# K of two batches mixed by 64x64 blocks in four array tiles, with a new order of work

## The chip, the cores and the metric

The kernel runs on one core of one Trainium2 chip. The metric is the device time of one execution in microseconds (us).

## What is computed

Inputs are q, k, v (4 batches, 8 heads, 768 rows, 64 columns), a sort network (4, 8, 8, 8) and the weights of a gated layer. The reference, cut to what matters:

```python
P = sort_net                                   # (4, 8, 8, 8)
for _ in range(5):
    P = exp(P - max(P)); P = P / (sum over j); P = P / (sum over i)
k_sorted = einsum('bhij,bhjcd->bhicd', P, k in 8 blocks of 96 rows)   # v_sorted likewise
attn = softmax(q_block @ k_sorted_block.T / 8)                        # 8 blocks of 96x96 per head
x = (attn @ v_sorted_block), heads side by side                       # (4, 768, 512)
h = maximum(x @ w_in, 0);  u, v = halves of h                         # 512 columns each
v_s = w_spatial @ layernorm(v) + b_spatial                            # (768 x 768) @ (768 x 512)
out = (u * v_s) @ w_out                                               # (4, 768, 512)
```

## The kernel before

All of the program is one list, `ORDER`, of small units. A unit is a name and its arguments; what it issues goes to the engines' queues in the order of the list, and each engine takes its own queue in order. Nothing is moved by a scheduler. `ps` arguments name the place in PSUM (0 to 3: two banks, 10 to 17: one bank), `A`, `D` and `P` an engine (ScalarE or ACT, VectorE or DVE, GpSimd or POOL). The units that matter here:

- `L` loads a tensor through POOL's DMA queue (`L:wu` and `L:wv` the input weights, L185 and L182, `L:wsa`, `L:wsb` the spatial weights, `L:wo` the output weights).
- `KT` (line 395 in `mixed`) mixes and turns K of one pair of heads: `pd`, a 128x128 matrix per head made on POOL (`PD`, line 293) from the normalised P and a mask, is multiplied with K as it lies in SBUF. Twelve matmuls of 128 columns, 64 array columns each; a copy by ACT or DVE puts the result into `kt_all`. `VM` (line 422) mixes V, `VC` copies it by eight DMAs on SyncE (SP) into `vb`.
- `QP` and `QX` turn q of batches 2 and 3 by a DMA transpose on SP (line 382); batches 0 and 1 are turned on TensorE (PE).
- `SC` (line 454) makes scores on PE (64 array rows) and their exponent on ACT; `AT` (line 500) multiplies with mixed V on PE, and DVE divides (a reciprocal, line 507, and a multiply, line 508). `XD` turns the result by a DMA transpose on SP (line 518), `XT` on PE.
- `VP` and `VH` (line 567) make the v half of the input product and its relu, `VP` in matmuls of 512 columns, `VH` in two of 256. `ST` (lines 587, 588), `LN` and `LA` (line 599) normalise it on DVE. `UP` (line 613) makes the u half.
- `WT`, `WW` turn the spatial weights on PE. `SP` (line 625) and, for batch 3, `SH` (line 681) are the spatial products, whose sum `z` DVE makes; all six normalised tiles of a batch feed each of them. `GT` and `GH` multiply with u on DVE or POOL; `OP` and `OH` (lines 651, 701) are the output products, `OE`, `OI` their copies, `OS`, `OJ` the stores.
- `CK` (lines 731 to 734) tests the sums of the softmax against a range with eleven small DVE operations, `CF` adds up the test on PE, `LF` loads the flag into every engine. `IF` is a branch on it: the rest of the list, or a general path that does not run for these inputs.

The list interleaves the batches: while batch b is in its gated layer, batch b+1 is in its attention.

Of the kernel before, what the change touches and what calls it, by code (L numbers as in the profile page):

```python
# [22 lines left out]
SC:0:0:0:0 L:v:1:0:8 PD:1:0:4 VB:15:D:0:3 SC:3:0:1:0 AT:1:0:2:0 SC:0:0:2:1 AT:2:0:3:0 SC:3:0:0:1 PD:1:4:8 AT:1:0:0:0  # L23
KT:0:A:1:0 XT:14:D:0:0:2 AT:3:0:0:1 SC:1:0:3:1 KT:0:A:1:3 AT:2:0:2:1 VM:1:A:1:0 AT:3:0:3:1 VM:0:A:1:1 VM:2:D:1:3
L:q:1:0:8 VM:1:A:1:2 XT:16:A:0:1:2 L:wv AT:0:0:1:0 XT:17:A:0:1:0 KT:2:D:1:1 KT:1:A:1:2 QT:16:D:1:1 QT:10:D:1:3
QT:11:A:1:2 QT:17:D:1:0 XT:14:D:0:0:0 SC:1:1:1:0 L:wsa SC:0:1:2:1 SC:3:1:2:0 VP:15:D:0:4 ST:0:4 VP:14:D:0:3 L:wu
SC:1:1:0:0 SC:0:1:1:1 VP:15:D:0:1 L:wsb ST:0:3 WT:16:A:1 WT:17:D:0 VP:14:A:0:0 ST:0:1 VH:15:A:0:2 ST:0:0 WT:16:A:2
VC:1:0:4 L:q:2:0:8 VH:17:A:0:5 VC:1:4:8 PD:2:0:4 ST:0:2 ST:0:5 AT:1:1:0:0 LN:0:0:6 AT:0:1:1:0 UP:2:A:0:0:0
UP:3:A:0:1:0 BI LA:0:3 LA:0:4 AT:1:1:2:0 SC:2:1:0:1 UP:0:A:0:1:1 LA:0:1 AT:3:1:2:1 L:v:2:0:8 WT:14:A:3 L:k:2:0:8
LA:0:5 LA:0:2 WW:1:D:4 LA:0:0 SC:0:1:3:1 SC:3:1:3:0 UP:2:A:0:0:1 PD:2:4:8 AT:0:1:3:1 QP:A:2:0 SP:1:0:3 QP:A:2:3  # L30
AT:3:1:3:0 QP:A:2:2 AT:2:1:0:1 QP:A:2:1 SP:0:0:0 AT:1:1:1:1 SP:3:0:2 VM:2:A:2:2 XD:1:0 VM:0:A:2:1 GT:D:0:0 SP:1:0:1
VM:3:D:2:0 GT:P:0:1 VM:2:A:2:3 VH:10:A:1:0 ST:1:0 KT:1:A:2:0 KT:2:D:2:1 KT:3:A:2:3 QX:2:0:4 KT:0:D:2:2 XD:1:1
UP:1:A:1:1:0 VH:16:D:1:1 SC:2:2:2:0 SC:0:2:0:0 VC:2:0:4:0:4 ST:1:1 GT:P:0:2 SC:1:2:3:0 VH:17:D:1:3 L:wo UP:2:A:1:1:1
AT:0:2:2:0 VH:16:A:1:4 AT:1:2:0:0 GT:P:0:3 VH:17:D:1:5 SC:2:2:1:0 L:q:3:0:8 SC:0:2:0:1 SC:1:2:1:1 VH:16:A:1:2 ST:1:3
UP:2:A:1:0:0 ST:1:5 AT:0:2:3:0 ST:1:4 ST:1:2 UP:1:A:1:0:1 LN:1:0:6 OP:3:0:2:2 LA:1:5 LA:1:1 SC:2:2:3:1 L:v:3:0:8
SC:0:2:2:1 PD:3:4:8 LA:1:0 OP:1:0:4:2 PD:3:0:4 LA:1:3 LA:1:2 OE:A:0:2 LA:1:4 L:k:3:0:8 QP:D:3:0 VC:2:4:8:0:4 OE:A:0:4
AT:2:2:3:1 SP:0:1:3 QP:A:3:3 AT:3:2:1:0 AT:1:2:2:1 QP:A:3:1 SP:2:1:1 AT:0:2:1:1 QP:A:3:2 VM:3:A:3:1 OP:1:0:0:2
OE:D:0:0 OS:0:0:0:1:A OS:0:0:1:2:A VM:2:A:3:3 AT:3:2:0:1 SP:0:1:2 VM:1:A:3:0 GT:P:1:1 XD:2:0 VM:3:D:3:2 SP:2:1:0
VH:16:D:2:2 QX:3:0:4 KT:0:A:3:0 KT:1:D:3:2 KT:2:D:3:3 KT:3:A:3:1 XD:2:1 VH:10:D:2:0 SC:1:3:0:1 ST:2:2 SC:3:3:0:0
SC:2:3:3:1 VC:3:4:8:0:4 OS:0:4:0:1 OS:0:4:1:2 VH:11:D:2:4 VH:10:A:2:5 AT:1:3:0:1 GT:P:1:3 VH:16:D:2:3 ST:2:3 ST:2:5  # L40
GT:P:1:2 SC:2:3:1:1 SC:0:3:2:1 SC:1:3:1:0 VH:17:A:2:1 GT:D:1:0 UP:2:A:2:1:0 AT:0:3:2:1 UP:1:A:2:1:1 ST:2:1 AT:3:3:1:1
ST:2:4 AT:2:3:3:1 UP:0:A:2:0:1 ST:2:0 UP:1:A:2:0:0 VC:3:0:4:0:4 AT:3:3:0:0 LN:2:0:6 LA:2:2 OP:0:1:0:2 OE:A:1:0 LA:2:4
AT:2:3:1:0 OP:1:1:4:2 LA:2:5 SC:3:3:2:0 LA:2:0 LA:2:3 LA:2:1 SC:0:3:3:0 OP:2:1:2:2 AT:3:3:3:0 SP:0:2:1 GT:D:2:1
OE:A:1:4 XD:3:1 AT:1:3:2:0 SP:3:2:0 SP:0:2:2 CK XD:3:0 GT:P:2:0 OE:A:1:2 SP:2:2:3 VH:1:D:3:5:3 GT:D:2:3 VH:10:D:3:4
UP:3:A:3:1:1 CF:11 VH:12:A:3:2 VH:13:A:3:1 OS:1:2:0:1 OS:1:2:1:2 LF VH:16:A:3:0 GT:D:2:2 OS:1:0:0:1:A OS:1:0:1:2:A
UP:2:A:3:1:0 ST:3:1 ST:3:3 UP:0:A:3:0:0 ST:3:4 ST:3:5 OP:1:2:0:2 ST:3:2 ST:3:0 OP:3:2:4:2 LN:3:0:6 LA:3:3 OE:D:2:0
LA:3:4 OP:2:2:2:2 LA:3:0 LA:3:1 OE:A:2:2 LA:3:5 UP:0:A:3:0:1 OE:A:2:4 LA:3:2 OS:0:2:0:1 OS:0:2:1:2 SH:12:3:2:0
SH:13:3:3:0 GH:P:3:3:0 SH:16:3:0:0 GH:D:3:2:0 SH:17:3:1:0 GH:P:3:0:0 SH:16:3:1:1 SH:12:3:2:1 OS:2:4 GH:P:3:1:0
SH:13:3:3:1 OS:2:0 GH:D:3:1:1 SH:17:3:0:1 OS:1:4 GH:D:3:3:1 OS:2:2 GH:P:3:0:1 GH:P:3:2:1 IF OH:16:3:2:0:512:0:4
# [19 lines left out]
def kernel(  # L69
# [18 lines left out]
    TB = 128 // NB  # L88
    BH = B * H
# [63 lines left out]
    prep_sb = const.tile([128, NB, BH], BF16, name="prep_sb")  # L153
    vm = const.tile([128, G, H, VW], BF16, name="vm")
# [16 lines left out]
    def u_L(what, *a):  # L171
        if what in ("q", "k", "v"):
# [113 lines left out]

    def u_PC(eng):
        copy(eng, prep_sb, st["pr"])
# [34 lines left out]
    def q_turned(t, b, hp):  # L323
        for g in range(G):
            for hh in range(2):
                nc.tensor.transpose(  # L326
                    t[hh * 64:hh * 64 + 64, g * 128:(g + 1) * 128],
                    st["q", b][:, 2 * hp + hh, g * D:(g + 1) * D], ident)
# [40 lines left out]
    def u_QP(eng, b, hp):  # L369

        b, hp = int(b), int(hp)
        if ("qp", b) not in st:
            st["qp", b] = ld_tile("qp").rearrange("p h c -> p (h c)").rearrange(
                "p (k g h d) -> p k g h d", k=HP, g=G, h=2)
        copy(
            eng, st["qp", b][:, hp].rearrange("p g h d -> p h g d"),
            st["q", b][:, 2 * hp:2 * hp + 2].rearrange("p h (g d) -> p h g d", g=G),
        )
# [23 lines left out]
    def u_KT(ps, eng, b, hp):  # L402
        mixed("k", "kT", ps, eng, int(b), int(hp))

# [41 lines left out]
    def u_SC(ps, b, hp, ih):  # L446
# [3 lines left out]
        for ii in range(NI):  # L450
            i = ih * NI + ii
            for hh in range(2):
                rows = slice(hh * 64, hh * 64 + 64)
# [9 lines left out]
    def u_SM(b, hp, ih):  # L463
# [5 lines left out]
        for ii in range(NI):  # L469
            i = ih * NI + ii  # L470
            for hh in range(2):
                rows = slice(hh * 64, hh * 64 + 64)
# [203 lines left out]
    def u_SH(ps, b, mc, c):  # L676
        b, mc, c = int(b), int(mc), int(c)
        t, x = ps_tile(ps)[:, 0], tokens(c)
        w = x.stop - x.start
        for n in range(G):  # L680
            nc.tensor.matmul(  # L681
                t[:, 0:w], lhsT=st["v_sb", b, n][:, mc * 128:(mc + 1) * 128],
                rhs=wspT[:, x.start // 128:x.stop // 128, n, :],
                start=(n == 0), stop=(n == G - 1),
            )
# [74 lines left out]
    def general_path():  # L760
# [9 lines left out]
        u_PC("A")  # L770
        for b in range(B):
            if b > 0:
                u_PD(b, 0, 8)
            for x in ("q", "k", "v"):
                u_L(x, b, 0, H)
# [3 lines left out]
            for hp in range(HP):  # L779
                u_QN(2, "A", b, hp)  # L780
                u_KT(3, "D", b, hp)
# [67 lines left out]
```

## Time and profile before

| | us |
|---|---|
| runs | 149.42, 150.09, 150.87 |
| median | 150.09 |
| span of the profiled execution, first to last instruction | 147.7 |
| PE busy | 141.4 |
| DVE busy | 115.1 |
| ACT busy | 85.2 |
| POOL busy | 39.1 |

The execution that was profiled has no time of its own listed beside its span; the runs' median is 2.4 us above that span, for what lies around the first and the last instruction. Of a page's lines: PE is TensorE's matmuls, PEld its weight loads, L625 a line of the kernel; a group's row gives its shapes, its count, busy time and mean duration in ns, then the engine's idle time ahead of it and what ended it.

### The profile page before, as it was taken

To read this page: it belongs to the slowest core of one execution; us is meant where nothing else is said; L and a number is where in the kernel's file an instruction comes from. 1 tells how busy PE (TensorE), PEld (TensorE's weight loads), DVE (VectorE), ACT (ScalarE), POOL (GpSimd) and SP (SyncE) were. 2 spreads that over 40 slices of the span, in tenths; PEclk is the share of its full clock that TensorE was granted. 3 is DMA by queue.
4 is the path that set the end of the run, shared out by engine and by line. 5 is a ranking of instruction groups with operands and counts; after the bars stand their busy time and mean duration, and the time that the engine had idled before them with its cause. 6 is when DMAs were issued, how large, how long until landed. Compare 5 with 4: busy or idle time off the path is not lost.

```text
span 147.7 us, 4114 instructions
## 1 busy us (share of the span) xinstructions
PE 141.4 (96%) x1691; PEld 101.0 (68%) x1691; DVE 115.1 (78%) x263; ACT 85.2 (58%) x125; POOL 39.1 (26%) x44
## 2 busy tenths in 40 slices
PE   6997999999999999999999999999999999999991
PEld 2466777857776667776877678768866876854760
DVE  3878899979987978867869879899558989846741
ACT  5357998988789447658793328756640046160040
POOL 6701994410000006991002640000002100004630
PEclk9999999999999999999999999999999999999999
DMA  2999999999999999899999999503602507007856
GB/s 60 278 204 205 204 207 201 208 225 243 227 233 231 204 200 269 131 177 211 206 202 175 213 239 278 132 0 83 28 0 60 190 2 284 0 2 266 307 210 228
DMA packets 37013, 25.93 MB, mean 176 GB/s; under 512 B 16704, under 2 KB 34112, under 8 KB 36992
## 3 DMA queue, kind: packets, MB, share of 16 engines
q0 software_dynamic: 14432, 12.19, 51.9%
q1 hardware_dynamic: 21552, 11.88, 33.8%
q10 hardware_dynamic: 1008, 1.57, 2.8%
q8 instruction: 14, 0.23, 0.6%
q14 instruction: 7, 0.06, 0.1%
HBM read 24.78 MB, written 6.29 MB: 210 GB/s over the span
## 4 chain that ended last, share of the span: by engine, by line
PE 82%; DMA 8%; DVE 5%; POOL 2%; issue 1%; ACT 1%; POOLq 0%; DVEq 0%
PE ps L625 16%; PE ps L567 15%; PE ps L613 14%; PE ps L651 11%; DMA k_in<-in_k_dram 8%; PE ps L681 5%; PE ps L500 4%; PE ps L395 4%; PE ps L701 4%; PE ps L454 4%; PE ps L422 3%; DVE x_sb L508 2%; PE ps L326 1%; PE ps L536 1%; PE ps L530 1%; DVE vb L124 1%
## 5 line engine op out<-in xcount | busy, mean ns | idle before, releaser
L642 POOL TENSOR_TENSOR gt<-z,u_sb 128x768 bf16<-128x768 f32 x7 | 11.4, 1642 | 68.0 <-DVE z L631 54.7
L459 ACT ACTIVATE ex_all<-ps 96x768 bf16<-96x768 f32 x32 | 23.7, 805 | 5.0 <-PE ps L454 4.1
L625 PE MATMUL ps<-wspT,v_sb 128*128 128x384 bf16 x144 | 25.0, 326 | 0.0
L567 PE MATMUL ps<-w_in_sb,xT 128*128 128x256 bf16 (+1 forms) x176 | 23.8, 283 | 0.0
L613 PE MATMUL ps<-xT,w_in_sb 128*128 128x384 bf16 x128 | 23.0, 326 | 0.0
L128 ACT ACTIVATE u_sb<-ps 128x768 bf16<-128x768 f32 x16 | 13.0, 811 | 17.3 <-PE ps L613 17.2
L508 DVE TENSOR_TENSOR x_sb<-ps,rec_all 96x512 bf16<-96x512 f32 x32 | 22.0, 687 | 1.1
L625 PEld LDWEIGHTS <-v_sb 128*128 128x128 bf16 x144 | 13.5, 98 | 8.4
L567 PEld LDWEIGHTS <-xT 128*128 128x128 bf16 x176 | 16.2, 98 | 4.0
L651 PE MATMUL ps<-w_out_sb,gt 128*128 128x256 bf16 x144 | 16.9, 273 | 0.0
L613 PEld LDWEIGHTS <-w_in_sb 128*128 128x128 bf16 x128 | 12.0, 98 | 7.0
L587 DVE BATCH_NORM_STATS2 stats<-v_sb 128x6 f32<-128x512 bf16 x24 | 16.2, 675 | 0.6 <-ACT v_sb L128 0.5
L122 ACT COPY o_sb<-ps 128x1024 f32<-128x1024 f32 (+2 forms) x11 | 8.9, 830 | 12.6 <-PE ps L701 9.3
L631 DVE TENSOR_TENSOR z<-ps,b_bc 128x768 f32<-128x768 f32 x12 | 11.5, 954 | 5.9 <-PE ps L625 5.1
L651 PEld LDWEIGHTS <-gt 128*128 128x128 bf16 x144 | 13.8, 98 | 2.0
L500 PEld LDWEIGHTS <-ex_all 96*128 96x128 bf16 x256 | 11.1, 97 | 2.6
L500 PE MATMUL ps<-vb,ex_all 96*128 96x65 bf16 x256 | 12.4, 193 | 0.1
L122 ACT CAST vm<-ps 128x768 bf16<-128x768 f32 x9 | 6.8, 807 | 9.7 <-PE ps L422 6.6
L694 POOL TENSOR_TENSOR gt<-z,u_sb 128x512 bf16<-128x512 f32 (+1 forms) x5 | 5.2, 1046 | 21.5 <-DVE z L687 21.5
L507 DVE RECIPROCAL rec_all<-ps 96x8 f32<-96x8 f32 x32 | 6.3, 196 | 5.5 <-PE ps L500 5.3
L130 DVE TENSOR_SCALAR v_sb<-ps 128x512 bf16<-128x512 f32 (+1 forms) x12 | 8.7, 727 | 1.7 <-PE ps L567 1.5
L236 PE MATMUL ps<-warm 128*128 128x512 bf16 (+3 forms) x38 | 8.5, 386 | 1.3 <-DVE warm L210 1.3
(100 smaller groups left out, 199.9 us busy)
## 6 DMA issues: line engine op xcount, KB each, us to landing
v_in<-in_v_dram POOLq DMA_DIRECT2D x4, 768.0 KB, 16.0
k_in<-in_k_dram POOLq DMA_DIRECT2D x4, 768.0 KB, 14.9
vb<-vm SPq DMA_DIRECT2D x24, 99.0 KB, 4.8
q_in<-in_q_dram POOLq DMA_DIRECT2D x3, 768.0 KB, 11.6
out_dram<-o_sb SPq DMA_DIRECT2D x9, 256.0 KB, 2.3
out_dram<-o_sb SPq DMA_DIRECT2D x4, 512.0 KB, 5.9
out_dram<-o_sb ACTq DMA_DIRECT2D x5, 256.0 KB, 2.3
ws_in<-in_moe_w_spatial_dram POOLq DMA_DIRECT2D x2, 576.0 KB, 18.9
```

What stands on the lines that cost most here:

```text
L122: nc.scalar.copy(out=out, in_=in_)
L128: nc.scalar.activation(out=out, in_=in_, func=AF.Relu)
L459: nc.scalar.activation(out=e_tile(b, hp, ih).rearrange("p h (x g) -> p h x g", g=G), in_=t[0:BLK, :, 0:HW].rearrange("p h (g x) -> p h x g ...
L500: nc.tensor.matmul(t[:, hh, ii * VW:ii * VW + D + 1], lhsT=e[:, c:c + 128], rhs=vb[b % 2][:, ih * NI + ii, 2 * hp + hh, 0:D + 1], start=Tr ...
L508: nc.vector.tensor_mul(out=x_sb[:, hp].rearrange("p i (h d) -> p h i d", h=2), in0=tv[:, :, :, 0:D], in1=_raw_ap(rec, 0, [rec.ap[0], [NI, ...
L567: nc.tensor.matmul(t[:, x, c:c + DH // parts], lhsT=st["xT", b][:, n // 3, kc, (n % 3) * 128:(n % 3 + 1) * 128], rhs=w_in_sb[:, kc, DH + c ...
L587: nc.vector.bn_stats(out=stats, in_=st["v_sb", b, n])
L613: nc.tensor.matmul(t[:, x, 0:HW], lhsT=w_in_sb[:, kc, mc * 128:(mc + 1) * 128], rhs=st["xT", b][:, ih, kc, :], start=(kc == 0), stop=(kc = ...
L625: nc.tensor.matmul(t[:, x, 0:HW], lhsT=st["v_sb", b, n][:, mc * 128:(mc + 1) * 128], rhs=wspT[:, 3 * x:3 * x + 3, n, :], start=(n == 0), s ...
L631: nc.vector.tensor_add(out=z.rearrange("p (x c) -> p x c", x=2), in0=t[:, :, 0:HW], in1=b_bc.rearrange("p (x c) -> p x c", x=2),)
L642: eng.tensor_mul(out=gt, in0=st["z", b, mc], in1=u)
L651: nc.tensor.matmul(t[:, x, c:c + w], lhsT=st["gt", b, mc][:, (n0 + x) * 128:(n0 + x + 1) * 128], rhs=w_out_sb[:, mc, c:c + w], start=(mc = ...
```

## The change

K of batches 2 and 3 is loaded in another layout: each partition holds 12 rows of one head, the 64 lower partitions an even head, the 64 upper ones an odd head, in 3 KB pieces in place of 1.5 KB. Eight blocks and 8 rows of each are mixed by a 64x64 matrix per head, `pn`, which two new POOL products (`PN`) make. For it stand new units: `M8` (two small POOL operations: a mask and a spread of 8 in place of 16), `PS` (eight matmuls that spread P for the last two batches) and `PY` (their copy by ACT). `KP` takes the place of `KT` there: for two pairs of heads 48 matmuls of 64 rows, 64 array columns and 64 columns each, turn by turn in four 64x64 tiles of the array, and two copies. In these batches odd pairs of heads have their two heads swapped in the partitions (`half`), so that `QP` copies an odd pair in two pieces.

The core of the diff:

```diff
+        if what == "k" and int(a[0]) >= KB:
...
+            nc.gpsimd.dma_start(
+                out=st["k", b][:, lo:hi],
+                in_=_raw_ap(k, (b * H + 2 * lo) * S * D, [[GR * D, 128], [2 * S * D, hi - lo], [1, GR * D]]),
+            )
...
+    def u_M8():
+        nc.gpsimd.tensor_add(out=mask8, in0=m32[:, 0:TR], in1=m32[:, TR:TB])
+        nc.gpsimd.tensor_copy(out=spread8, in_=spread[:, :, 0:TR])
+
+    def u_PS(ps):
...
+        for i in range(NI):
+            for hh in range(2):
+                nc.tensor.matmul(
+                    parts[hh * 64:hh * 64 + 64, i], lhsT=spread8[:, i * NB:(i + 1) * NB].rearrange("p j t -> p (j t)"),
+                    rhs=turned_p[:, hh, :, KB * HP:], start=True, stop=True,
+                )
...
+    def u_PN(b, lo, hi):
...
+        nc.gpsimd.tensor_mul(
+            out=pn(b)[:, lo:hi].rearrange("p h (i t) -> p h i t", t=TR),
+            in0=_raw_ap(mask8, 0, [mask8.ap[0], [0, n], [0, NB], [1, TR]]),
+            in1=_raw_ap(prep8, (b - KB) * HP + lo, [prep8.ap[0], [1, n], [(B - KB) * HP, NB], [0, TR]]),
+        )
+
+    def half(b, hp, hh):
+        lo = 64 * (hh ^ (hp & 1) if b >= KB else hh)
+        return slice(lo, lo + 64)
...
+    def u_KP(ps0, ps1, eng, b, m):
+        b, m = int(b), int(m)
+        ts = [ps_tile(ps0), ps_tile(ps1)]
+        for n in range(GR):
+            for row in range(2):
+                g = (n + G * row) % GR
+                for o in range(2):
+                    rows = slice(64 * row, 64 * row + 64)
+                    nc.tensor.matmul(
+                        ts[o][half(b, o, row), g // G, (g % G) * 64:(g % G) * 64 + 64],
+                        lhsT=st["k", b][rows, 2 * m + o, g * D:(g + 1) * D], rhs=pn(b)[rows, 2 * m + o, :],
+                        start=True, stop=True,
+                    )
+        for o in range(2):
+            to = turned("kT", b, 2 * m + o)[:, 0:S].rearrange("p (x b g) -> p b x g", b=2, g=G)
+            copy(eng[o], to, ts[o][:, :, 0:HW].rearrange("p b (g x) -> p b x g", g=G))
```

(GR = 12, G = 6, KB = 2.) The list `ORDER` is another one from the middle of batch 1's attention on: nearly every unit behind it has another place or another engine. Two of its lines, before and after:

```diff
-VH:16:D:2:2 QX:3:0:4 KT:0:A:3:0 KT:1:D:3:2 KT:2:D:3:3 KT:3:A:3:1 XD:2:1 VH:10:D:2:0 SC:1:3:0:1 ST:2:2 SC:3:3:0:0
+QP:D:3:2 QX:3:0:4 SP:3:1:2 SP:0:1:1 KP:2:3:DA:3:0 GT:P:1:1 VH:12:D:2:0 VH:10:A:2:1 VH:15:A:2:4 VH:14:A:2:2 GT:D:1:2
```

Among the units that change places: the first `UP` of batch 0 stands ahead of its two neighbouring attention products instead of behind them; `XD:2:1`, the second half of batch 2, ahead of `QX:3` instead of behind it; `CK` behind the first V product of batch 3 instead of ahead of it; `L:wo` behind three `GT` on POOL instead of two; DVE has five `UP` copies (none before) and three `GT` in place of five.

On SyncE's queue, before, from batch 2's copies of mixed V on (`vb` is the mixed V, `qT` and `xT` the turned q and attention result):

```order
L435 DMA vb_97<-vm 96x1x528 x8
L518 DMA_TRANSPOSE xT<-x_sb 128x16x96
L382 DMA_TRANSPOSE qT<-qp 128x24x128
L518 DMA_TRANSPOSE xT<-x_sb 128x16x96
L435 DMA vb_98<-vm 96x1x528 x4
L666 DMA out_dram<-o_sb 128x512 x2
L435 DMA vb_98<-vm 96x1x528 x4
```

The same place now:

```order
L505 DMA vb_100<-vm 96x1x528 x8
L588 DMA_TRANSPOSE xT<-x_sb 128x16x96 x2
L435 DMA_TRANSPOSE qT<-qp 128x24x128
L505 DMA vb_101<-vm 96x1x528 x8
L736 DMA out_dram<-o_sb 128x512 x2
```

The turned q of batch 3 went behind the second `xT` of batch 2, and the copies of V are no longer parted by stores.

On DVE, before, from batch 2's last spatial sum (`z`) on, right behind the eleven operations of `CK` (`v_sb` a relu copy of V, `gt` a product with u, the two `ends` and `flag` rows the end of the range check):

```order
L631 TENSOR_TENSOR z<-ps,b_bc 128x768
L130 TENSOR_SCALAR v_sb<-ps 128x1024
L642 TENSOR_TENSOR gt<-z,u_sb 128x768
L130 TENSOR_SCALAR v_sb<-ps 128x512
L748 TENSOR_REDUCE ends<-ps 1x1
L749 CAST flag<-ends 1x1
L752 TENSOR_LOAD flag
L642 TENSOR_TENSOR gt<-z,u_sb 128x768
L587 BN_STATS stats<-v_sb 128x6
L588 BN_AGGR mv<-stats 128x2
```

The same place now, from the V copy of two tiles on, as far as the first operations of `CK`:

```order
L133 TENSOR_SCALAR v_sb<-ps 128x1024
L133 TENSOR_SCALAR u_sb<-ps 128x2x384
L657 BN_STATS stats<-v_sb 128x6
L658 BN_AGGR mv<-stats 128x2
L803 MEMSET bad 128x5
L805 TENSOR_REDUCE ends<-rec_all 96x1
L806 TENSOR_SCALAR bad<-ends 96x1
```

And what stands behind `CK`:

```order
L133 TENSOR_SCALAR v_sb<-ps 128x512
L657 BN_STATS stats<-v_sb 128x6
L658 BN_AGGR mv<-stats 128x2
L133 TENSOR_SCALAR u_sb<-ps 128x2x384
L712 TENSOR_TENSOR gt<-z,u_sb 128x768
```

`CK` and two U copies came in between batch 3's V copies and statistics; one `gt` and the load of the flag went out of this place.

130 lines of the change are left out of this document (81 added, 49 removed).

## The prediction

> **What bounds the kernel now.** I read the page first: its span, its busy times and the shares of its chain.
>
> ```profile
> span 147.7 us, 4114 instructions
> PE 141.4 (96%) x1691; PEld 101.0 (68%) x1691; DVE 115.1 (78%) x263; ACT 85.2 (58%) x125; POOL 39.1 (26%) x44
> PE 82%; DMA 8%; DVE 5%; POOL 2%; issue 1%; ACT 1%; POOLq 0%; DVEq 0%
> ```
>
> TensorE holds 82% of the chain that ended last, but a busy PE need not be a PE at its pace. So I looked in the view of waits for everything PE itself waited for, and then at busy time by stretches (their columns: length, then busy time and count of PE, PEld, DVE, ACT, POOL, then the granted clock, DMA share and GB/s).
>
> ```profile
> PE ps L236 <- DVE warm L210: 1.3, 1, 1.3
> PE ps L413 <- ACT vt_all L122: 0.6, 1, 0.6
> PE ps L267 <- DVE mask L224: 0.5, 1, 0.5
> 90.00:105.00 15.00, 15.00 (x194) 11.61 (x188) 14.00 (x34) 10.14 (x15) 0.00 (x0) 1.00 0.52 99
> 115.00:125.00 10.00, 10.00 (x80) 7.50 (x78) 8.76 (x23) 3.51 (x6) 0.01 (x1) 1.00 0.44 163
> ```
>
> These three are all of PE's own waits, and they belong to the start: warm-up, the mixing weights, the first turn of V. In the stretches shown, as in all between 30 and 125 us, PE has something to do in every moment, at full granted clock. So in that stretch the time is the sum of PE's work, and the change can help only by making that sum smaller. It can hurt in two ways: more PE work, or the first waits of PE. Also to be seen: DVE is next, with 14.0 of 15 us and 8.8 of 10 us in two of the stretches.
>
> **The head.** Up to 30 us the list of work is the same in both kernels but for two small POOL operations, ahead of loads that queue behind earlier transfers anyway. The two belong to M8 and are smaller than this product of POOL's, the nearest one:
>
> ```profile
> L293 POOL TENSOR_TENSOR pd<-mask,prep_sb 128x512 bf16<-128x512 bf16 x6 | 6.5, 1105 | 7.6 <-ACT prep_sb L122 7.6
> ```
>
> I cost the head at nothing; without that cover it is up to 1.1 us.
>
> **PE's sum.** The chain in order of time gives PE's price per piece (start, length, what, count):
>
> ```profile
> 27.34 0.34 PE ps L530 x8
> 34.30 0.67 PE ps L536 x12
> 37.91 0.48 PE ps L500 x16
> 56.98 1.46 PE ps L395 x48
> 58.44 1.41 PE ps L613 x8
> 59.84 0.87 PE ps L567 x8
> 60.72 0.62 PE ps L454 x24
> 61.34 0.98 PE ps L567 x8
> 68.99 1.30 PE ps L613 x8
> 81.85 1.95 PE ps L625 x12
> 87.33 1.46 PE ps L395 x48
> 131.41 7.80 PE ps L681 x48
> ```
>
> First, a change of the array's shape costs 0.1 us: eight L567 take 0.87, but 0.98 behind the score products (L454, 64 rows); eight L613 take 1.30, but 1.41 behind the K mixing (L395, 64 columns). Counting such changes in the two lists of work from 30 us on, I find 26 before and 32 after: the K mixing stands in four places instead of two, PS adds one change, and the scores stand in one more group. That is +0.6 us.
>
> Second, the K mixing of batches 2 and 3. Before it is 2 x 1.46, less 0.1 each for the shape: 2.7 us for 96 matmuls of 128 columns, 28 ns each. A matmul of 128 columns on the whole array takes 56 ns (0.67 / 12), so two half tiles run at once. The score products agree: (0.62 - 0.1) / 24 = 22 ns, against 42 (0.34 / 8) for 96 columns on the whole array. After it is 192 matmuls of 64 columns and 64 rows, 48 rounds of four tiles. No row shows four tiles. A matmul of 65 columns takes 30 ns (0.48 / 16). So the mixing costs 48 x 30 = 1.4 us if all four run at once, 96 x 30 = 2.9 if only two do, 192 x 30 = 5.8 if none do. Both half-tile shapes overlap fully in these rows, so I go near the first end, with 10% for the starts: 1.6, that is -1.1 us (ends -1.3 and +3.0).
>
> [...]
>
> Third, PS: eight matmuls of few columns, 0.1 to 0.25 us, taken as +0.15. That V products come in one piece of 512 instead of two of 256 changes nothing (both stream the same columns). PE's sum: -1.1 + 0.6 + 0.15 = -0.35 us (ends -0.6 and +3.8).
>
> **The waits that the new list brings.** Here I looked for who is late next.
>
> The input weights (wu, L185) are issued at 18.59 and land 19.3 later, at 37.9. The first product that reads them is L613:
>
> ```profile
> 37.75 0.65 PE L500 MATMUL ps<-vb,ex_all 96*128 96x65 bf16 x16
> 38.23 2.77 PE L613 MATMUL ps<-xT,w_in_sb 128*128 128x384 bf16 x16
> ```
>
> ```profile
> L185 POOL DMA_DIRECT2D w_in_sb<-in_moe_w_in_dram x1: 810/810/810, 18.6 to 18.6; - x1
> DMA to landing us min/median/max: 19.3/19.3/19.3
> ```
>
> In the new list two attention products (0.48) and one turn of weights (0.34) that stood ahead of it come behind it, and PS and its shape come ahead (0.25): PE is there at 38.23 - 0.82 + 0.25 = 37.66. The loads ahead of wu in its queue are the same. So PE waits 0.3 (0 to 0.5).
>
> Batch 3's turned queries come by a DMA transpose in SyncE's queue:
>
> ```profile
> 78.52 1.59 SPq L518 DMA_TRANSPOSE xT<-x_sb  x1
> 80.20 3.86 SPq L382 DMA_TRANSPOSE qT<-qp  x1
> ```
>
> ```profile
> DMA to landing us min/median/max: 6.4/7.4/8.5
> ```
>
> ```profile
> 89.70 0.75 PE L454 MATMUL ps<-qT,kt_all 64*128 64x96 bf16 x24
> ```
>
> The second fence is L382's. Before, qT is issued at 80.20, lands at 88.7, and the first scores of batch 3 come at 89.7: 1 us to spare. After, batch 2's second xT stands ahead of it in SyncE's queue, and waits until the last second-half attention product of batch 2 (AT:1:2:3:1) is divided and stored. From that product's end on PE: 0.1 hand-over, reciprocal and multiply on DVE (0.20 + 0.69, rows below), 1.7 for the xT on SyncE (78.52 to 80.20), then 7.4 to landing: 10.1 us. PE meanwhile has two spatial products, five V products, two mixings and four shapes: 2 x 1.95 + 5 x 0.87 + 2 x 0.4 + 0.4 = 9.45. PE waits 0.65 (0 with 6.4, 1.75 with 8.5). Queued behind qT on SyncE are batch 3's eight V copies (VC); the attention products that read them come after the scores, so they are late only as much as these.
>
> The largest is on DVE, between the last spatial product of batch 2 and the first of batch 3:
>
> ```profile
> 114.50 0.41 DVE L733 TENSOR_REDUCE ends<-rec_all 96x1 f32<-96x256 f32 x1
> ```
>
> ```profile
> 116.26 0.96 DVE L631 TENSOR_TENSOR z<-ps,b_bc 128x768 f32<-128x768 f32 x1
> 117.31 1.22 DVE L130 TENSOR_SCALAR v_sb<-ps 128x1024 bf16<-128x1024 f32 x1
> 118.45 0.95 DVE L642 TENSOR_TENSOR gt<-z,u_sb 128x768 bf16<-128x768 f32 x1
> 119.31 0.68 DVE L130 TENSOR_SCALAR v_sb<-ps 128x512 bf16<-128x512 f32 x1
> 120.90 0.96 DVE L642 TENSOR_TENSOR gt<-z,u_sb 128x768 bf16<-128x768 f32 x1 [0.67 <-DVE flag L749]
> 122.06 0.69 DVE L587 BATCH_NORM_STATS2 stats<-v_sb 128x6 f32<-128x512 bf16 x1 [0.20 <-ACT v_sb L128]
> 129.02 1.70 DVE L599 TENSOR_SCALAR v_sb<-v_sb,mv,rstd 128x512 bf16<-128x512 bf16 x5
> ```
>
> Before, DVE works from 117.31 (the two-tile V copy) to 130.72 (the last normalisation): 13.4 us. The first spatial product of batch 3 (L681) starts at 131.41, 0.7 later, so DVE just keeps up. After, PE's work in this section is the same (four V products, four U products, three output products), but DVE gets the range check into it, which ran in 114.50 to 116.26 before (1.76), and two U copies of 768 that ACT did (0.86 each from start to start, as 118.45 to 119.31 for the same size). It loses one gt (0.86), the 0.67 pause for the flag and the 0.20. So 13.4 + 1.76 + 1.72 - 0.86 - 0.87 = 15.15 us, 1.75 more than before, against 0.7 to spare. All six normalised tiles feed every spatial product, so PE waits 1.1 (0.7 if a U copy takes no longer than the 0.68 of the 512 one, 1.6 if DVE has 0.4 us of work left over when the section begins).
>
> Last, smaller places: the first spatial products of batches 0 and 1 now need a normalised tile that DVE writes within two attention products (0.48) ahead of them, and three products reuse a PSUM bank that DVE empties now (U copies given to DVE). Each can cost nothing or one DVE operation:
>
> ```profile
> L508 DVE TENSOR_TENSOR x_sb<-ps,rec_all 96x512 bf16<-96x512 f32 x32 | 22.0, 687 | 1.1
> L507 DVE RECIPROCAL rec_all<-ps 96x8 f32<-96x8 f32 x32 | 6.3, 196 | 5.5 <-PE ps L500 5.3
> ```
>
> Five places at 0 to 0.3: 0.7, half of 1.5. ACT has room (85 us); the new POOL operations (M8, PN) run while POOL idles.
>
> **The sum.** -0.35 + 0.3 + 0.65 + 1.1 + 0.7 = +2.4 us. The profiled execution's span is 147.7; the three runs have a median of 150.09, 2.4 more, for what lies around the span and the run it was. So the span becomes 150.1 and the time 152.5.
>
> **Rivals.** (1) DVE's work is covered, and PE's sum decides: in the section ahead of batch 3's spatial products DVE fits once more into what PE gives it. The point is 14.1 us (13.4 + 0.7): under it PE does not wait there, and the small places, which are DVE's too, go with it. What is left is -0.35 and up to 0.95 for wu and qT, or -0.6 with neither: 149.5 to 150.7, not slower. For it: PE waited for nothing before, with DVE at 14.0 of 15 us in one stretch. Against it: I count 15.15 there, from measured rows. Truly faster by 1% would need 1.5 us out of a PE sum that has 0.6 to give. (2) The four tiles don't run four at once. Two at once: the mixing costs 2.9, +1.3 on the forecast, less what waits shrink: 153.7. (3) Four small tiles take their turns, each matmul with a start of its own as on the whole array (30 ns): the mixing costs 5.8, +4.2 on the forecast, of which PE's later arrival takes off the 0.65 for qT: 156. [...] That the mixing isn't moved to four tiles at all is excluded: PE's list has 192 matmuls of 64x64 in place of 96 of 64x128.
>
> **How the numbers follow.** Forecast 0.58 (151.2 to 154.3: the ends of its terms, not all at once), rival 1 0.26, rival 2 0.11, rival 3 0.05. Within 1% of 150.09 (148.6 to 151.6, about what a measurement of this kernel can tell from no change) lie rival 1 but for 0.05 and a little of the forecast: 0.24; faster 0.05; slower 0.71. The range takes in rival 1's lower end but for little, and reaches up to rival 3: 149.9 to 155.5.
>
> **What would show it.** The K mixing (four groups of 48) at 0.4 us each plus 0.1; eight L613 behind them at 1.4. Among PE's waits: one for w_in_sb near 38, one for qT near 93, one for the normalised tiles ahead of the first L681's counterpart, about 1 us, with DVE busy without a gap for 15 us there. I am wrong if PE shows no wait ahead of that product, if a mixing takes 0.7 or more, or if the first 30 us differ.

## The result, and the profile after

The changed kernel takes 158.43 us in the median (156.84 to 159.24, six runs), the kernel before 150.15 (149.40 to 153.82) beside it: a ratio of 1.055 (95% interval 1.050 to 1.060). The forecast was 152.5 (149.9 to 155.5): the direction came true, the size did not, and the time lies outside the forecast's range.

The page of the changed kernel, whose profiled execution is the slowest of the six, 159.24 us (the granted clock by fortieths of the span stands in the third line):

```profile
span 157.4 us, 4272 instructions
...
PE 144.5 (92%) x1767; PEld 99.0 (63%) x1767; DVE 117.3 (75%) x268; ACT 81.6 (52%) x124; POOL 43.1 (27%) x49
...
PEclk9999999999999999975899999999999999999999
...
PE 50%; DMA 38%; DVE 5%; POOL 3%; issue 2%; ACT 1%; POOLq 0%; DVEq 0%
```

TensorE's share of the chain fell from 82% to 50%, DMA's rose from 8% to 38%, and the clock, whole throughout before, drops in three slices between 67 and 79 us. All six executions of the changed kernel show a mean clock of 0.978 to 0.989, so the drop is its own, though not equally long in each. The view of waits, for PE:

```profile
PE ps L570 <- DMA vb<-vm: 4.0, 2, 2.1
...
PE ps L524 <- DMA qT<-qp: 1.1, 1, 1.1
```

Before, PE waited for nothing between 30 and 125 us. Now it waits 4.0 us for two copies of mixed V (`vb`) and 1.1 for batch 3's turned queries. PE's timeline at the place of the first (start, length, what; in brackets the idle time and what ended it):

```profile
65.83 0.23 PE L570 MATMUL ps<-vb,ex_all 96*128 96x65 bf16 x2
67.97 0.19 PE L570 MATMUL ps<-vb,ex_all 96*128 96x65 bf16 x1 [1.92 <-DMA vb<-vm]
70.25 0.44 PE L570 MATMUL ps<-vb,ex_all 96*128 96x65 bf16 x5 [2.09 <-DMA vb<-vm]
...
71.38 2.74 PE L683 MATMUL ps<-xT,w_in_sb 128*128 128x384 bf16 x8
73.91 1.09 PE L570 MATMUL ps<-vb,ex_all 96*128 96x65 bf16 x16
74.81 2.02 PE L683 MATMUL ps<-xT,w_in_sb 128*128 128x384 bf16 x8
```

The product `AT:0:2:3:0` starts at 65.83, does the two sixteenths whose copies have landed, and stands for the third copy until 67.97 and for the fourth until 70.25. The eight U products behind it then take 2.74 us and the next eight 2.02, against 1.41 to 1.46 elsewhere. Busy time and granted clock by stretches (after the count of POOL: clock, DMA share, GB/s) say why:

```profile
65.80:70.30 4.50, 0.49 (x7) 0.29 (x6) 0.19 (x1) 0.60 (x1) 1.55 (x2) 0.87 1.15 183
70.30:73.00 2.70, 2.70 (x27) 1.62 (x27) 1.67 (x4) 1.50 (x2) 0.00 (x0) 0.50 1.26 238
73.00:77.00 4.00, 4.00 (x32) 2.58 (x31) 1.76 (x5) 0.81 (x1) 0.00 (x0) 0.63 1.32 205
77.00:82.00 5.00, 5.00 (x72) 4.31 (x69) 4.21 (x11) 3.98 (x7) 0.00 (x0) 1.00 1.06 186
```

After 4.5 us in which PE worked 0.49, the mean clock is 0.50 for 2.7 us and 0.63 for 4 more. The 0.63 is a mean of two: by the trace's record the clock was 0.50 from 69.1 to 76.0 us, 6.8 us in one piece, and whole on both sides.

```profile
69.20:75.90 6.70, 5.65 (x49) 3.56 (x49) 2.84 (x8) 2.31 (x3) 0.00 (x0) 0.50 1.27 221
```

From the end of the wait on that is 2.7 x 0.50 + 4.0 x 0.37 = 2.8 us of work not done. So in this execution PE lost 4.0 + 2.8 + 1.1 = 7.9 us in three places, of which the forecast had one, at 0.65.

Why the copies came late, by the queues of SyncE and POOL around them, before and after:

```profile
51.80 4.27 SPq L382 DMA_TRANSPOSE qT<-qp  x1
...
57.59 5.70 SPq L435 DMA_DIRECT2D vb<-vm  x8
```

```profile
59.79 0.82 POOL L194 DMA_DIRECT2D w_out_sb<-in_moe_w_out_dram  x1
```

```profile
54.21 3.77 SPq L435 DMA_TRANSPOSE qT<-qp  x1
...
59.52 7.07 SPq L505 DMA_DIRECT2D vb<-vm  x8
```

```profile
61.27 0.81 POOL L208 DMA_DIRECT2D w_out_sb<-in_moe_w_out_dram  x1
62.06 0.89 POOL L191 DMA_DIRECT2D v_in<-in_v_dram  x1
```

Before, the four copies that the first attention products of batch 2 need were issued from 57.59 to 59.74, the fourth just ahead of POOL's output weights (59.79); the four landed by 62.95, and the first product came at 63.45. That is half a microsecond to spare. Now the copies start at 59.52, and the third and fourth are issued at 61.61 and 62.82, behind the weights (61.27) and the next V (62.06). The chain shows what the fourth pays for it:

```profile
62.82 7.39 DMA vb<-vm
```

7.4 us instead of the 3.2 that the fourth took before. In this trace the two copies issued ahead of the loads land 4.1 and 2.9 us after their issue, the six behind them 6.3 to 8.2. So a copy issued behind loads of 512 and 768 KB seems to wait for them; the first run below tests it.

### The profile page after: what moved, and what is told of

It is laid out like the page before. It is cut to its first block, busy times and chain, and to the rows that moved or that the text cites. A ratio compares the mean times of both kernels' runs of the same rounds, so it can differ in the third digit from the quotient of the medians.

```text
span 157.4 us, 4272 instructions
## 1 busy us (share of the span) xinstructions
PE 144.5 (92%) x1767; PEld 99.0 (63%) x1767; DVE 117.3 (75%) x268; ACT 81.6 (52%) x124; POOL 43.1 (27%) x49
## 4 chain that ended last, share of the span: by engine, by line
PE 50%; DMA 38%; DVE 5%; POOL 3%; issue 2%; ACT 1%; POOLq 0%; DVEq 0%
DMA b_bc<-in_moe_b_spatial_dram 16%; DMA v_in<-in_v_dram 12%; PE ps L695 12%; PE ps L721 10%; PE ps L683 9%; DMA qT<-qp 5%; PE ps L753 5%; DMA vb<-vm 5%; PE ps L773 3%; PE ps L637 3%; PE ps L570 3%; PE ps L524 2%; PE ps L492 2%; DVE u_sb L133 1%; POOL k_in L191 1%
## 5 line engine op out<-in xcount | busy, mean ns | idle before, releaser
L712 POOL TENSOR_TENSOR gt<-z,u_sb 128x768 bf16<-128x768 f32 x9 | 14.8, 1645 | 66.9 <-DVE z L701 54.4
L683 PE MATMUL ps<-xT,w_in_sb 128*128 128x384 bf16 x128 | 25.3, 344 | 0.1
L695 PE MATMUL ps<-wspT,v_sb 128*128 128x384 bf16 x144 | 25.1, 326 | 0.0
L637 PE MATMUL ps<-w_in_sb,xT 128*128 128x256 bf16 (+1 forms) x148 | 22.9, 304 | 0.0
L131 ACT ACTIVATE v_sb<-ps 128x512 bf16<-128x512 f32 x15 | 8.9, 597 | 17.4 <-PE ps L637 17.3
L637 PEld LDWEIGHTS <-xT 128*128 128x128 bf16 x148 | 14.1, 98 | 5.7
L125 ACT COPY o_sb<-ps 128x1024 f32<-128x1024 f32 (+2 forms) x12 | 10.0, 843 | 12.8 <-PE ps L773 9.1
L131 ACT ACTIVATE u_sb<-ps 128x768 bf16<-128x768 f32 x11 | 8.9, 810 | 8.0 <-PE ps L683 4.4
L127 DVE CAST kt_all<-ps 128x768 bf16<-128x768 f32 x8 | 7.5, 951 | 4.0 <-ACT v_sb L131 2.0
L524 PE MATMUL ps<-qT,kt_all 64*128 64x96 bf16 x256 | 9.1, 208 | 1.4 <-DMA qT<-qp 1.1
```

The costliest lines, as they stand in the source:

```text
L125: nc.scalar.copy(out=out, in_=in_)
L131: nc.scalar.activation(out=out, in_=in_, func=AF.Relu)
L524: nc.tensor.matmul(t[:, hh, 0:HW].rearrange("p (g x) -> p g x", g=G)[:, :, ii * TB:(ii + 1) * TB], lhsT=kT[rows, i * BLK:i * BLK + 128], r ...
L637: nc.tensor.matmul(t[:, x, c:c + DH // parts], lhsT=st["xT", b][:, n // 3, kc, (n % 3) * 128:(n % 3 + 1) * 128], rhs=w_in_sb[:, kc, DH + c ...
L683: nc.tensor.matmul(t[:, x, 0:HW], lhsT=w_in_sb[:, kc, mc * 128:(mc + 1) * 128], rhs=st["xT", b][:, ih, kc, :], start=(kc == 0), stop=(kc = ...
L695: nc.tensor.matmul(t[:, x, 0:HW], lhsT=st["v_sb", b, n][:, mc * 128:(mc + 1) * 128], rhs=wspT[:, 3 * x:3 * x + 3, n, :], start=(n == 0), s ...
```

## The experiments

### Is it the wait for V, and the clock behind it?

First run: POOL reads one element of each of the four copies ahead of its three loads, so the loads can't overtake.

```diff
+    def u_WV(b, lo, hi):
+        nc.gpsimd.tensor_copy(out=gate[:, int(lo):int(hi)], in_=vb[int(b) % 2][0:1, int(lo):int(hi), 0, 0:1])
-... L:wo L:v:3:0:8 L:q:3:0:8
+... WV:2:0:4 L:wo L:v:3:0:8 L:q:3:0:8
```

> The changed kernel, but POOL reads a word of each of the first four V copies of batch 2 before it issues the loads of the output weights and of batch 3's v and q, so that these loads start after the copies have landed (a new tiny POOL operation; nothing is left out). Theory A (the copies run into the loads): the third and fourth copy land about 3 us after their issue instead of 6.3 and 7.4, by 66 us; PE's wait for them (4.1 us) shrinks to under 0.5, its clock stays at 1.00, and the time falls by 4.3 + 2.5 to about 152; up to 1 us may come back because batch 3's loads come 3 us later. Rival B (the copies are late because SyncE issues them late, the loads have no part in it): the wait stays above 3 us, 157 to 159.

Measured 153.65 us (153.16 to 154.02), ratio 1.021 (1.011 to 1.031), clock 1.0. The third and fourth copy, issued as late as before, land 3.3 and 2.8 us after their issue: it was the loads that held them. The wait for `vb` is gone and the clock whole, as expected; the time is a good 1.5 us above the expected 152, for the held-back output weights are late now, and batch 3's queries as before:

```profile
PE ps L725 <- DMA w_out_sb<-in_moe_w_out_dram: 1.2, 1, 1.2
PE ps L528 <- DMA qT<-qp: 0.9, 1, 0.9
```

Second run: the loads stay where they are, and 19 products of 512 columns that nobody reads fill PE's wait.

```diff
-AT:0:2:3:0
+DM:0:19:512 AT:0:2:3:0
```

> The changed kernel with 19 matmuls of zeros, 512 columns each (4.1 us of PE), ahead of the attention product that waits for the V copies; their result is overwritten. Theory A (PE's pause halves its clock, which costs 2.5 us more): PE's work and wait fill the same time up to 70.3 us, the clock stays at 1.00 behind it, eight L683 take 1.3 us instead of 2.67, and the time falls by about 2.5 to 156. Rival C (the products from 70 to 77 us are slow because of the transfers then under way): no change, 158 to 159.

Measured 154.88 us (154.76 to 155.05), ratio 1.029 (1.020 to 1.039). The copies land as late as ever, but the clock behind them stays whole:

```profile
69.90:72.50 2.60, 2.54 (x48) 1.82 (x45) 1.67 (x4) 1.77 (x3) 0.00 (x0) 1.00 1.25 239
```

So 3.55 us came back with no change but work in the wait: the 2.8 of the clock, and 0.7 at batch 3's queries (their wait fell from 1.1 to 0.4). The clock is shown as a cost of its own, though more came back than the run's expectation gave it (2.5).

### Which half of the change is it?

Third run: the order of before, with K of batches 2 and 3 on four tiles. Fourth: the new order, with K as before.

```diff
 # the tiles alone, in the order of before
-KT:1:A:2:0 KT:2:D:2:1 KT:3:A:2:3 QX:2:0:4 KT:0:D:2:2
+KP:1:2:AD:2:0 QX:2:0:4 KP:0:3:DA:2:1
...
 # the order alone, in the code of before
-KP:3:0:DD:2:1
+KT:3:D:2:2 KT:0:D:2:3
```

> The kernel before with the K mixing of batches 2 and 3 in four array tiles alone: its own order of work, each K unit replaced where it stands, and the units that prepare it put in. Theory A (the mixing gains what it should, the order loses): 96 matmuls of 128 columns, 2.7 us, become 1.6, PS and its change of shape cost 0.25, so -0.85: 149.3 (148.8 to 149.8). Rival D (the four tiles lose by themselves): 150.5 or more.

> The new order of work with the old K mixing: each four-tile unit replaced by two old ones in its place, the units that prepare it left out. Theory A (the loss is the order's): PE's wait for the V copies and the halved clock are there as in the changed kernel, 157.5 to 159.5 (the mixing costs 1.1 more, of which 0.5 falls into the wait). Rival D (the loss is the four tiles'): 150.5 to 153.

Measured: the tiles alone 163.92 us (163.82 to 165.57), ratio 1.090 (1.080 to 1.100); the order alone 152.62 (152.45 to 152.76), 1.015 (1.006 to 1.024). My own theory, that the new order makes the copies late, fell in both: in the fourth run they are in time, in the third they are late by 3.4 us (and 3.5 more stand at the end, on which below). The other theory's 150.5 to 153 for the order alone came true, but it had no reason for a loss of 13 us with the tiles. In the fourth run PE's work ahead of the copies was nearly the same and SyncE began at the same moment:

```profile
51.91 1.80 SPq L518 DMA_TRANSPOSE xT<-x_sb  x1
53.90 3.05 SPq L382 DMA_TRANSPOSE qT<-qp  x1
...
58.45 5.40 SPq L435 DMA_DIRECT2D vb<-vm  x8
```

The first xT is issued at 51.9 in both, but q's transpose takes SyncE 3.05 us here and 3.77 in the changed kernel, and the eight copies 5.40 and 7.07. The DMAs do the same job and are slower in one program than in the other. By window (50 to 64 us; median us from issue to landing at the end of a row), the changed kernel and then the order alone:

```profile
xT<-x_sb SPq DMA_TRANSPOSE x2, 4.1
qT<-qp SPq DMA_TRANSPOSE x1, 5.8
```

```profile
vb<-vm SPq DMA_DIRECT2D x8, 99.0 KB, 3.2
...
xT<-x_sb SPq DMA_TRANSPOSE x2, 3.6
qT<-qp SPq DMA_TRANSPOSE x1, 4.6
```

All four kernels with the new code so far had the slow figure for this q, 5.7 to 5.9 us. (In the kernel before, the first transposes, issued from 50.08 on, queue behind a load whose packets run to 53.4 us, and can't be compared.) What the two codes do not share, besides the mixing itself, is where tiles lie: the change puts three small tables, of 128, 512 and 32 bytes per partition, among the constants, and every tile allocated behind them moves up by 672 bytes. In the built programs `qp`, `qT`, `x_sb` and `xT`, which the transposes read and write, start at multiples of 256 bytes before and 160 past one now (192 in the first run, which adds a small tile of its own).

### Is it the place of the tiles?

Fifth and eighth run: the changed kernel with one unused tile of 96 or of 32 bytes behind the tables. Ninth: the 96 bytes further back, behind the V tiles, so that these stay shifted and all tiles behind them, those of the transposes among them, return to their old remainder. Seventh: the kernel before with an unused tile of 672 bytes, and nothing else. The three edits of the diff are those of the fifth, the ninth and the seventh; the eighth has 16 elements in place of 48.

```diff
     mask8 = const.tile([128, TR], BF16, name="mask8")
+    pad = const.tile([128, 48], BF16, name="pad")
...
     vt_all = const.tile([128, 2, S + 32], BF16, name="vt_all")
+    pad = const.tile([128, 48], BF16, name="pad")
...
     prep_sb = const.tile([128, NB, BH], BF16, name="prep_sb")
+    pad = const.tile([128, 336], BF16, name="pad")
```

> The changed kernel with one unused tile of 96 bytes per partition behind the three new tables. The three tables (128, 512 and 32 bytes per partition) push every tile allocated after them, among them the source and target tiles of the transposing DMAs (qp, qT, x_sb, xT) and the V tiles, 672 bytes up: from places that are multiples of 64 and, for these, of 256 bytes to places 32 past a multiple of 64. The 96 bytes bring each back to its old remainder. Theory S (the shift slows the transposing DMAs: in the traces of the changed code xT lands 3.8 us after its issue and the q of batch 3 7.1 to 8.4 us, in the new order with K by two tiles, whose tiles stand where they stood before, 3.5 and 4.9): xT 3.5, q of batch 3 4.9, the third and fourth V copy of batch 2 land before POOL's loads bite, no wait of 4 us, no halved clock: 151.5 us (150.5 to 153). Rival W (the shift is nothing; the mixing on four tiles and its preparation delay SyncE in another way): 156.5 to 159, xT still 3.8.

> The changed kernel with 32 unused bytes per partition instead of 96: the tiles behind stand at multiples of 64 again, but 192 past a multiple of 256, not at it. Theory S64 (what counts is the remainder by 64): as with 96 bytes, 151.5 us (150.5 to 153), xT 3.5. Theory S256 (what counts is the remainder by 256): as the changed kernel, 156 to 159, xT 3.8. Rival W: 156 to 159 in both.

> The changed kernel with the 96 unused bytes per partition behind the V and exponential tiles instead of ahead of them: vm, vb, the exponentials and the turned K and V stay shifted by 672 bytes, while qp, qT, x_sb and xT, which the transposing DMAs read and write, are back at multiples of 256. Theory T (the shift costs through the transposes alone): as with all tiles back, 151.5 us (150.8 to 152.5), xT landing 3.5 us after issue, q of batch 3 4.9, copies of V in time. Rival V (the copies of V, which read and write the shifted tiles, are what is slow): 155 to 159, with the wait for vb there again; part of both: between.

> The kernel before, with nothing but one unused tile of 672 bytes per partition where the change puts its tables, so that all later tiles stand where they stand in the changed kernel. Theory S: xT and qT transposes slow by 0.3 us and 1 to 3 us, the V copies of batch 2 are issued about 1.4 us later and meet POOL's loads, which in this order are issued at 59.8: a wait of 2 to 4 us and a halved clock behind it, 156 us (152 to 162). Rival W: an unused tile costs nothing, 150 (149.4 to 151).

| run | transposes' tiles, past a multiple of 256 | us (range) | ratio (interval) |
|---|---|---|---|
| changed kernel | 160 | 158.43 (156.84 to 159.24) | 1.055 (1.050 to 1.060) |
| with 96 bytes | 0 | 151.54 (151.05 to 151.57) | 1.011 (1.006 to 1.016) |
| with 32 bytes | 192 | 158.56 (158.29 to 159.59) | 1.058 (1.053 to 1.063) |
| 96 bytes behind V | 0 | 151.40 (151.11 to 151.98) | 1.011 (1.003 to 1.018) |
| before, with 672 bytes | 160 | 156.79 (156.08 to 157.87) | 1.047 (1.039 to 1.055) |

All four times came out as the theory of the shift had it, in the eighth run in its form with 256; of the landings that it named, batch 3's q came at 6.5 and 6.4 us in the fifth and ninth run, not at 4.9. An unused tile of 96 bytes takes 6.9 us off the changed kernel, and one of 672 bytes puts 7.0 us on the kernel before (149.79 beside it). That settles the cause of these 6.9 us. The remainder by 64 does not matter (the transposes' tiles of the run with 32 bytes are at multiples of 64, and it is as slow as without); the transposes are fast with their tiles at multiples of 256 and slow at 160 and 192 past one; and for V it does not matter, which may stay shifted (151.40 us). The same window in the run with 96 bytes, then with 32:

```profile
vb<-vm SPq DMA_DIRECT2D x8, 99.0 KB, 3.3
...
xT<-x_sb SPq DMA_TRANSPOSE x2, 3.5
qT<-qp SPq DMA_TRANSPOSE x1, 4.6
```

```profile
vb<-vm SPq DMA_DIRECT2D x5, 99.0 KB, 7.6
xT<-x_sb SPq DMA_TRANSPOSE x2, 4.1
qT<-qp SPq DMA_TRANSPOSE x1, 5.7
```

And the pages' rows of that queue (packets, MB, the packets' time as a share of 16 engines' span), 96 bytes first:

```profile
q1 hardware_dynamic: 21552, 11.88, 30.3%
```

```profile
q1 hardware_dynamic: 21552, 11.88, 31.8%
```

The same packets and bytes take 30.3% of 149.7 = 45.4 us in one and 31.8% of 157.7 = 50.1 in the other, 11% more. Sorted by size, the traces' packets tell whose time this is: the queue's 15,392 packets of 256 bytes, all but 32 of them the transposes', take 18.6 ns in the mean with 96 bytes and 23.0 with 32, and the 2304 packets of 1056 bytes, the V copies', 82.7 and 82.8; the 2176 of the output stores, 2048 bytes each, 84.9 and 88.2. POOL's loads into shifted tiles take no longer either (q0 on the pages: 50.1% of 149.7 = 75.0 us, 47.7% of 157.7 = 75.2). So nearly all the time that the shift adds is the transposes' own: 68 of the 76 us, counted over 16 engines. The runs show fast transposes with the tiles at multiples of 256 bytes and slow ones at 160 and 192 past one; why, they do not show, nor whether source or target does it, nor whether multiples of 128 would do.

The kernel before with 672 bytes has the late copies and the halved clock in a program whose order nobody touched (PE's waits, then clock and busy time at that place):

```profile
PE ps L501 <- DMA vb<-vm: 3.8, 2, 2.8
```

```profile
68.00:71.00 3.00, 3.00 (x22) 2.26 (x20) 1.59 (x4) 0.60 (x1) 0.00 (x0) 0.50 1.26 234
```

The way there was not quite the expected one. Its transposes land no later after their issue than those of before (q 6.3 us and 6.4, the xT ahead of the copies 3.8 and 3.8), but SyncE is held longer: 4.9 us instead of 4.3 in issuing q, 1.3 instead of 0.7 in issuing the first copy. So the third copy is issued at 60.2 instead of 59.1, behind POOL's output weights (59.65), and takes 6.1 us. Half a microsecond of room was all that the kernel before had.

### Would the four tiles pay in the old order?

Sixth run: the tiles alone, with the 96 bytes. Tenth: with other places for the spreading and the mixings as well (the diff is the tenth's, cut to two places, against the kernel before).

```diff
-VP:15:D:0:4 ST:0:4
+VP:15:D:0:4 PS:17 PY:A ST:0:4
...
-KT:0:A:3:0 KT:1:D:3:2 KT:2:D:3:3 KT:3:A:3:1 XD:2:1 VH:10:D:2:0
+KP:0:1:AD:3:0 XD:2:1 VH:10:D:2:0 KP:3:2:DA:3:1
```

> The kernel of the run with the tiles alone (the order of before, K of the late batches on four tiles), with the same 96 unused bytes per partition. Theory S: the tile shift was what cost there too, so the V copies of batch 2 land in time and the clock stays whole; what is left is the sum of the four-tile mixing, near the time before: 150 us (149 to 152.5). Rival W: 161 to 165 as without the bytes. If the time falls only to about 158, the stall at the end (output products that waited 3.5 us for POOL) is a cost of its own.

> The order of before with K of the late batches on four tiles, all tiles at their old remainders (96 unused bytes), the spreading of the table ahead of the two turned weights on its bank, each pair of mixings on the banks that come free first, and batch 2's first V product of one sixth between the two pairs of the last batch. Sum: the mixing saves 1.1 us of PE time, 0.15 are spent on the spreading, and in the late batch 2 the saved 0.5 us may be lost to the transposed q that lands where it landed: 149.3 us (148.8 to 151) against about 150. Rival: PE or SyncE is late by some tenths at the third batch's head, copies of V fall behind POOL's loads as in the two runs with the tiles alone, and it is 153 to 158.

Measured: 158.10 us (156.63 to 161.62), ratio 1.049 (1.041 to 1.056), and 158.26 (156.68 to 158.69), 1.055 (1.050 to 1.061). Both miss the sum. The sixth has the 158 that its expectation named for a stall at the end, in part by luck, since the copies were late as well; the tenth is near its rival's number, but by another way. In the sixth the spreading waited 0.5 us for a bank, SyncE began 0.8 us later than before, the fourth copy again fell behind POOL's loads (2.5 us of wait), and batch 3's mixing waited 0.7 for its second bank. In the tenth no copy was late, but PE waited for banks all the same, up to 1.0 us at a place. So whether the tiles pay in the old order stays open. And both, like the third run, stand at the end, behind the branch (the tenth, in the timeline):

```profile
146.23 5.37 PE L774 MATMUL ps<-w_out_sb,gt 128*128 128x512 bf16 x36 [2.86 <-POOLq L895]
```

The releaser named is POOL's queue at the branch, but the last product that this matmul reads from POOL was there at 143.0. What the three runs share is the length of PE's program ahead of the branch. Counting PE's instructions in the built programs, the code that the branch jumps to begins behind 7399 others, those of the path that it jumps over among them, in all three, and behind 6979 and 7341 in the kernels before and after, which do not stand there. (With the second run's 19 more products and their weight loads it is 7379, and that run does not stand either.) Theory P: the place of this code decides. Rival Q: the order of the work does. Eleventh run: the tenth with ten early filling products made thirty with the same columns, so that the code begins behind 7439. Twelfth: the changed kernel with 96 bytes, its ten made 39, so that it begins behind 7399 in place of 7341.

```diff
-DM:13:10:192
+DM:13:30:64
...
-DM:13:10:192
+DM:13:39:48
```

> The run before with the order of before and the tiles placed (158.3 us; its output products behind the range check wait 2.9 us for nothing but the branch), with ten early filling products of 192 columns made 30 of 64: the same columns, 40 TensorE instructions more ahead of the branch. [...] Rival Q (the stall is of the order of the work, such as a late POOL): 157.5 to 159.

> [...] Theory P: the first output products wait 2.5 to 3.5 us behind the branch, 154.5 us (153.8 to 155.5). Rival Q: 151.5 (151 to 152.3).

Measured: 154.60 us (154.32 to 155.88), ratio 1.032 (1.023 to 1.041): 3.7 less than the tenth, where P had 155.2 (154.5 to 156), and the stall is gone. (Some of the 3.7 is clock: six of the tenth's seven executions show a mean of 0.989, three of the eleventh's four 1.00.) The twelfth has the stall, in a program that did not have it (the eleventh's line first):

```profile
143.87 5.37 PE L774 MATMUL ps<-w_out_sb,gt 128*128 128x512 bf16 x36
```

```profile
142.31 5.38 PE L774 MATMUL ps<-w_out_sb,gt 128*128 128x512 bf16 x36 [1.91 <-issue]
```

Its time, 152.43 (151.88 to 152.78), ratio 1.014 (1.006 to 1.022), is only 0.9 above the run without, between the two forecasts, and the intervals of the two ratios overlap; by the trace the stall is 1.9 us, less than I expected. What decides is the branch itself, which the traces list in PE's queue (duration in ns, start), the fifth run's first, then the twelfth's:

```profile
L895 PEldq COMPARE_BRANCH  x1: 396/396/396, 137.7 to 137.7; - x1
```

```profile
L895 PEldq COMPARE_BRANCH  x1: 3960/3960/3960, 138.3 to 138.3; - x1
```

It takes 4.0 to 5.1 us in the four runs that stand and 0.4 to 0.5 in the other ten programs. PE's sequencer comes to it ahead of the matmuls, and what PE has still queued hides a part: in the twelfth run the branch is done at 142.25 and the queued work at 140.40, which leaves the 1.9. In all these programs the branch jumps over more than 3600 instructions of PE, and ten of them do not stand. That the place of the code decides is shown by the two runs, for 7399 against 7439 and 7341; why, is not.

## Why the prediction was wrong

**Places of tiles: the step that was missing.** The part on the change went through operations, waits and queues. It gave the three new tables no term, as they are a few hundred bytes that nobody waits for. Their cost was the 672 bytes by which they moved the transposes' tiles: 158.43 - 151.54 = 6.9 us, more than the 5.9 by which the forecast was too low. Without the shift the changed kernel takes 151.5, inside the forecast's own range (151.2 to 154.3), 1.0 under its centre; but that is in part luck: of the four terms for waits only the input weights' came out without the shift, as shown below.

**V copies of batch 2: the step that would have caught it.** The prediction followed `VC` only behind batch 3's queries ("late only as much as these"). It took "PE waits for nothing" as room. The rows of before had a margin of 0.5 us at that place, between the landing of the fourth copy and the first product, and POOL's loads beside it; copies issued behind those loads took 6.5 to 7.7 us even then, unnoticed because nobody waited for them. A wait of 4 us there was a rival to be priced, whatever would make SyncE late. In this case a pause of this length then halved the clock, which belongs to its price. The step that failed is thus the cost of the V copies, put at nothing because PE did not wait for them before: the runs show 4.0 us of wait and 2.8 of halved clock there.

**K mixing: right.** Forecast 0.4 us for each of four groups, 0.1 for the shape. The chain of the changed kernel, and the same four heads on two tiles in the order alone:

```profile
56.93 0.51 PE ps L466 x48
```

```profile
56.97 0.79 PE ps L395 x24
```

0.51 for 48 matmuls of 64 columns, 8.5 ns each from the 0.41 without the change of shape, against the 30 that the prediction reads for one of 65 columns, so four tiles do run at once. (The chain has 0.71 for the second group, with the hand-over to the copy behind it; in PE's timeline both take 0.58.) Rivals 2 and 3 fall. The four groups saved 4 x (0.79 - 0.51) = 1.1 us, the figure of the forecast. Between the runs of the order alone and of the change with 96 bytes, which differ by the tiles, the medians differ by 1.1 too; by their ratios to the kernel before it is 0.4%, 0.6 us, and the intervals overlap.

**Input weights: right.** Forecast 0.3. The first product that reads them starts at 37.94, as the load lands:

```profile
37.31 0.50 PE L606 MATMUL ps<-ident,ws_in 128*128 128x128 bf16 x6
37.94 1.47 PE L683 MATMUL ps<-xT,w_in_sb 128*128 128x384 bf16 x8
```

The six turns of weights ahead of it are done at 37.65, by the 56 ns apiece of the prediction, so PE waits 0.3.

**Queries of batch 3: place right, reason wrong.** Forecast 0.65 from SyncE's queue; measured 1.1. With the tiles back in place q lands 6.5 us after its issue instead of 7.8, and PE waits nothing there. The 7.4 that I took was the mean of two transposes that both stood behind other transfers; in the order alone, behind none, batch 3's takes 4.9.

**DVE ahead of batch 3's spatial products: length right, wait wrong.** Forecast 15.15 us of DVE without a gap, and a wait of 1.1 for PE. DVE's first and last operation of the section, then PE's first spatial product:

```profile
125.66 1.23 DVE L133 TENSOR_SCALAR v_sb<-ps 128x1024 bf16<-128x1024 f32 x1 [0.70 <-PE ps L637]
```

```profile
138.80 2.03 DVE L669 TENSOR_SCALAR v_sb<-v_sb,mv,rstd 128x512 bf16<-128x512 bf16 x6 [0.61 <-ACT rstd L664]
```

```profile
140.00 2.36 PE L753 MATMUL ps<-wspT,v_sb 128*128 128x512 bf16 x10
```

From 125.66 to 140.83 are 15.17 us. That this is the forecast's 15.15 is in part luck, for it was to be work without a gap, and 0.61 of it is a pause in which DVE stands for ACT. PE goes on at 140.00 without a pause, when some three of the six normalised tiles are there (six take 2.03), and waits for the others as they come:

```profile
PEld L753 <- DVE v_sb L669: 0.5, 2, 0.2
```

Two short waits of the weight loads, 0.5 in all, and none of the matmuls: by the prediction's own sign ("no wait ahead of that product") this step was wrong. The step "all six feed every spatial product" is true, but a product of six matmuls needs them one after another, not all at its start.

**The small places.** Forecast 0.7; in the run with 96 bytes the largest that is left is a wait of 0.3 for a gated product.

In sum, without the shift the change costs 1.6 us (ratio 1.011), against a forecast of 2.4. Where the 1.6 lie is not worked out: PE's waits that this run has and the kernel before has not come to 0.5 (0.3 for the gated product, 0.2 for the input weights), besides the 0.5 of the weight loads above. The order alone costs 2.2 (1.015), of which the four tiles give back part. No run was faster than the kernel before.

## What to carry to other kernels

A new constant, however small, moves every tile behind it: before pricing a change, compare the tiles' places in the two programs, and keep what a DMA transposes at multiples of 256 bytes, where the transposes were fast (an unused tile of 96 bytes was worth 6.9 us here). An engine that never waits says nothing about margins: read for each transfer when it lands and when it is first needed, and which large load is issued just behind it, for 1.1 us of delay at the first V copy (58.4 to 59.5) became 4 us of wait and 2.8 of halved clock. And when one half of a change, run alone, refutes its own theory, look for what the two programs differ in besides the order of their work.

## What the runs showed of the hardware

- Transposing DMAs between SBUF tiles at 160 or 192 past a multiple of 256 bytes: in the new order of work, between 50 and 64 us, xT 4.1 us from issue to landing (median of two) instead of 3.5 to 3.6 with the tiles at such a multiple, q 5.7 to 5.8 instead of 4.6, and SyncE is held longer in issuing them (3.6 to 3.8 us against 3.0 for q). In the run with 32 bytes their packets of 256 bytes take 23.0 ns, with 96 bytes 18.6 (in the kernel before, at multiples of 256 too but in its other order of work, 25.1: the place is not all that sets them); those of the output stores (2048 bytes) 88.2 and 84.9, those of the V copies (1056 bytes) 82.8 and 82.7.
- A pause of PE of 4.5 us with 0.5 of work in it was followed by a granted clock of 0.50 for 6.8 us, and the like pauses of the third, seventh and eighth run by the same 6.8; filling the pause with products kept it at 1.00. Of the sixth run's two shorter pauses, one of 2.5 us left it whole and one of 2.4 was followed by 3.4 us at 0.50.
- Four tiles of 64x64 ran at once, 8.5 ns per matmul of 64 columns (0.41 us for 48, in the changed kernel).
- Where the code behind PE's branch begins behind 7399 of PE's instructions, the branch took 4.0 to 5.1 us and PE stood 1.9 to 3.5 (four runs); with 6922, 6979, 7341, 7379 or 7439 ahead of it the branch took 0.4 to 0.5 (ten programs).
